# Two attention blocks on one core: projections as rounds of four 32-column tiles, a scheduler with measured waits, GpSimd joins of up to four groups, patterns shifted downwards

## The chip, the core and the metric

The kernel runs on one core of one Trainium2 chip. The metric is the device time of one execution in microseconds (us), as the median of several runs. One execution was also taken with the hardware profiler; all rows below come from it. Engine names: PE is TensorE (matmuls; "PEld" its weight loads), ACT is ScalarE, DVE is VectorE, POOL is GpSimd, SP issues DMAs.

## What is computed

Two independent blocks, each on a sequence of 2048 rows with 512 features, 32 heads of width 16; their outputs are set side by side.

```python
qkv = (x @ wqkv).reshape(B, S, 3, H, Dh).transpose(2, 0, 3, 1, 4)   # S=2048, H=32, Dh=16
# block A, linear attention
phi = lambda t: jnp.where(t > 0, t + 1, jnp.exp(t)) + 1e-6
kv  = einsum("bhsd,bhse->bhde", phi(k), v);  z = sum of phi(k) over s
o   = (phi(q) @ kv) / (phi(q) @ z + 1e-6)
# block B, softmax attention
o   = softmax(q @ k.T * Dh**-0.5) @ v
# each: o in (B, S, D) @ wo;  result = concatenate([a, b], axis=-1)
```

Nearly all the time is block B: 32 heads times 2048 x 2048 scores, an exponential of each.

## The kernel before

**Units and blocks.** The heads of B are handled in 32 units: four head groups Gp, four stretches c of 512 queries, and two halves e_ of the group's heads, so that a unit holds four heads (g = 0 to 3). A unit has 64 blocks, one for each of 16 key tiles j and four heads g: 128 keys by 512 queries. There are 2048 blocks in all. For each one PE computes the scores (`qk`, L871, a matmul with 32 rows of the array, so up to four with different g run side by side), something makes the exponential, and PE multiplies the result with the values (L1253, 128 rows and a tile of 32 columns of the array, of which 17 are used: 16 value columns and a column of ones that gives the softmax's denominator). Four such matmuls with different g also run side by side; such a set is called a round.

**Two ways to the exponential.** The ACT way: PE writes two or three blocks into the PSUM tile pS, and one ACT instruction (L1084) writes their exponentials as fp16 into PT. The integer way: PE writes one block into a bank of pD (or the fifth bank of pS), and DVE (L987) makes an int16 of it, `score * ESC + EB`, whose bits read as fp16 are a rough exponential. Two more patterns are made of it by adding constants (`SHIFT`), 328 for pattern 1 and 656 for pattern 2. The weighted sum of the three is a good exponential, and PE makes it: three value matmuls for each block in place of one, pattern 0 with values multiplied by `VW` (tile VX), patterns 1 and 2 with the plain values VV. Blocks of the integer way are collected in groups of two (1024 columns; eight group buffers of the tile DI). Patterns 1 and 2 of a group are made by GpSimd (`on_pool`, L1176), where up to two waiting shifts are joined in one instruction; with both a pattern 1 and a pattern 2 in it, the pattern 2 is made of the group's finished pattern 1, with 328. Pattern 2 is made by DVE instead (`on_dve`, L1141) when GpSimd's backlog is long.

**The jobs.** Beside this run the projections of B (`proj_job` L600, `v4_job` L677), all of block A (`ak_job` and `av_job` L718, `aq_job` L755, `akvsum_job`, `aden_job`, `anum_job`), the two output projections (`omm_job` L809) and checks of the input's size (`gram_x`, `gram_w`, `flag_job`). The function `halves` cuts the matmuls of a job in two parts of equal length that are placed one by one. All use the full 128x128 array. Their PSUM results are evicted by DVE, or go through an exponential on ACT (L693) and two DVE instructions.

**The order.** Everything is one static program. When it is written, a list scheduler runs through a simulated time: it holds a clock `T` for each engine, a duration for each operation, latencies between engines (`LAT`, 0.12 us, and `LPE`), and always emits the candidate that can start first, by priorities. `fill_act_cand` offers the score matmuls for the next ACT instruction, `fill_d_cand` those for the integer way, `pv_cand` up to `PVR` rounds of value matmuls at once, `job_cand` a part of a job. A PE candidate is dropped if it would end after the time at which the next ACT fill has to start. How many blocks go the integer way is a result of this: a block goes there whenever a bank, a group buffer and the backlogs of DVE and GpSimd allow. The table `SEG` sets 25 parameters of the scheduler anew every 12 us of simulated time (windows, thresholds, priorities, a seed). The chip executes each engine's list in the emitted order, with semaphores where one engine needs another's result.

Of the kernel before, what the change touches and what calls it, by code (L numbers as in the profile page):

```python
# [238 lines left out]
def bass_concat_heads__linear_attn_block__softmax_full_mha__prompt_kernel(nc, A_x, A_wqkv, A_wo, B_x, B_wqkv, B_wo, out):  # L239
# [18 lines left out]
    VW = 1.5546875  # L258
    SHIFT = (328, 656)
    PMX = 0.0  # L260
# [64 lines left out]
    )  # L325
    GB = 0.0
    PM = -0.1
# [28 lines left out]
    EB = 13125.0  # L356
# [3 lines left out]
    with es:  # L360
# [164 lines left out]
        LAT = 0.12  # L525
        LPE = {"dve": 0.04, "act": 0.19, "pool": 0.0, "pe": 0.12, "dma": 0.12}
# [6 lines left out]
        class Shared(float):  # L533

            pass

# [8 lines left out]
        class Job:  # L545
# [11 lines left out]
            def stage_done(self, i, end, bk, bi):  # L557
# [3 lines left out]
                for st, tk in self.gives:  # L561
                    if st == i:
                        tok[tk] = end + LAT
                if i + 1 < len(self.stages):
                    eng, dur, fn = self.stages[i + 1]
                    lat = LAT if eng != "pe" or eng != self.stages[i][0] else 0.0
                    push(eng, end + lat, self.prio if eng == "pe" else (0 if eng == "act" or i + 1 <= self.rel and self.bank else min(self.prio, 2)), dur,
                         lambda st_, en_, fn=fn: (fn(bk), self.stage_done(i + 1, en_, bk, bi)))
# [10 lines left out]
        MM = 0.26  # L579
# [4 lines left out]

        def halves(fn, reads, n=4, parts=2, dur=MM):

            def mk(lo, hi):
                def f(e, bk):
                    for i in range(lo, hi):
                        ins = fn(e, bk, i)  # L590
# [896 lines left out]
        def fill_in(st):  # L1487
# [4 lines left out]
            if n <= 0:  # L1492
                return
# [188 lines left out]
```

## Time and profile before

| | before |
|---|---|
| runs | 661.0, 661.37, 660.76 us; median 661.0 |
| profiled execution | 660.98 us, span from first to last instruction 659.2 us |
| granted TensorE clock | 0.999 |
| ACT exponentials of B (L1084) | 648 instructions: 575 of two blocks, 73 of three, so 1369 blocks |
| integer way (L987) | 492 blocks from pD and 187 from pS, so 679 blocks |
| pattern shifts on GpSimd (L1176) | 198 of 128x2048, 169 of 128x1024, 2 of 128x512 |
| pattern shifts on DVE (L1141) | 113 |
| DMA | 21.53 MB in 53213 packets, mean 33 GB/s |

A row of a group reads: line, engine, operation, output <- input with shapes, count | busy time of the group in us, mean ns of one | idle time of the engine just before them and what ended it. A row of the timeline reads: start and length in us, engine, line, operation, tiles, count; like instructions that follow each other are merged, and the length is then from the first's start to the last's end. The records of PE, DVE and ACT contain the time to the last write, so that the next instruction starts before the record of the last has ended: the pace of an engine is read from the distance of starts, not from the mean length.

### The profile page before, as it was taken

What the parts mean: (1) busy time and instruction counts of PE and PEld (TensorE: products, weight loads), DVE (VectorE), ACT (ScalarE), POOL (GpSimd) and SP (SyncE); (2) the same over time, 40 slices, a digit from 0 to 9 for tenths busy, and PEclk for the clock granted to TensorE, in tenths of its full rate; (3) what the DMA queues carried; (4) which work ended last, traced back from release to release, by engine and by line L of the source; (5) the groups of instructions that cost most, each with busy time, mean ns of one, the idle gap of its engine ahead of it and who ended that gap; (6) DMA issues with size and microseconds to landing.
All of it is one profiled execution on the core that took longest, in us unless ns stands there. A gap on an engine that the chain in (4) does not pass through costs nothing.

```text
span 659.2 us, 15950 instructions
## 1 busy us (share of the span) xinstructions
PE 633.3 (96%) x6609; PEld 200.4 (30%) x6662; DVE 632.1 (96%) x1089; ACT 644.7 (98%) x686; POOL 592.7 (90%) x450
## 2 busy tenths in 40 slices
PE   8999999999999999999999999999999999999997
PEld 6323333222333333332222233322222223232222
DVE  4999999999999999999999999999999999999995
ACT  6999999999999999999999999999999999999994
POOL 5999999999999999999998899999999999999983
PEclk9999999999999999999999999999999999999999
DMA  9701010020102101210012011010011000120102
GB/s 178 207 3 33 1 34 6 11 43 9 34 2 33 21 14 33 65 34 9 9 27 64 17 34 34 18 19 10 7 26 41 17 1 11 25 26 25 33 26 67
DMA packets 53213, 21.53 MB, mean 33 GB/s; under 512 B 44177, under 2 KB 52625, under 8 KB 53137
## 3 DMA queue, kind: packets, MB, share of 16 engines
q1 hardware_dynamic: 51664, 19.80, 13.9%
q8 instruction: 54, 0.88, 0.6%
q10 hardware_dynamic: 1472, 0.66, 0.4%
q14 instruction: 23, 0.18, 0.1%
HBM read 4.46 MB, written 4.19 MB: 13 GB/s over the span
## 4 chain that ended last, share of the span: by engine, by line
ACT 96%; PE 3%; DMA 1%; ACTq 0%; issue 0%; DVE 0%; DVEq 0%
ACT PT L1084 93%; ACT EA L693 2%; DMA Wb<-in_B_wqkv_dram 1%; PE pPV L1253 1%; PE pD L809 1%; PE pS L871 0%; PE pD L1305 0%; PE pS L1305 0%; PE pS L1389 0%; ACTq L442 0%; PE pD L1389 0%; DVE KNa L582 0%; PE pD L659 0%; PE pD L871 0%; DVEq L1626 0%
## 5 line engine op out<-in xcount | busy, mean ns | idle before, releaser
L1084 ACT ACTIVATE PT<-pS 128x1024 f16<-128x1024 f32 (+1 forms) x648 | 636.6, 1305 | 1.0 <-PE pS L871 1.0
L1176 POOL TENSOR_SCALAR DI<-DI 128x2048 int16<-128x2048 int16 (+1 forms) x369 | 554.4, 1503 | 47.3 <-DVE DI L987 20.2
L987 DVE TENSOR_SCALAR DI<-pD 128x512 int16<-128x512 f32 x492 | 324.4, 679 | 6.1 <-PE pD L871 2.5
L871 PE MATMUL pS<-QT,KM 32*128 32x512 bf16 x1556 | 255.0, 384 | 8.8 <-ACT PT L1084 4.5
L1253 PE MATMUL pPV<-PT,VV 128*17 128x512 f16 x1369 | 233.7, 381 | 0.0
L1253 PE MATMUL pPV<-DI,VV 128*17 128x512 f16 x1358 | 227.3, 382 | 0.0
L871 PE MATMUL pD<-QT,KM 32*128 32x512 bf16 x492 | 170.5, 384 | 0.3 <-DVE PQT L696 0.3
L1253 PE MATMUL pPV<-DI,VX 128*17 128x512 f16 x679 | 161.0, 381 | 0.2 <-DVE OT L1282 0.2
L871 PEld LDWEIGHTS pS<-QT,KM 32*128 32x128 bf16 x1556 | 64.6, 91 | 265.3 <-ACT PT L1084 227.4
L987 DVE TENSOR_SCALAR DI<-pS 128x512 int16<-128x512 f32 x187 | 126.6, 677 | 0.7
L1141 DVE TENSOR_SCALAR DI<-DI 128x1056 int16<-128x1056 int16 x113 | 77.0, 687 | 0.5
L1253 PEld LDWEIGHTS pPV<-PT,VV 128*17 128x17 bf16 x1369 | 47.5, 88 | 41.4 <-issue 36.1
L1253 PEld LDWEIGHTS pPV<-DI,VV 128*17 128x17 bf16 x1358 | 47.0, 88 | 40.4 <-issue 33.0
L871 PEld LDWEIGHTS pD<-QT,KM 32*128 32x128 bf16 x492 | 40.5, 91 | 5.4 <-DVE DI L987 2.0
L1253 PEld LDWEIGHTS pPV<-DI,VX 128*17 128x17 bf16 x679 | 34.2, 88 | 22.0 <-issue 17.7
L718 PE MATMUL pD<-Wa,xTa 128*128 128x256 bf16 x200 | 30.5, 275 | 0.3 <-DVE DI L987 0.2
L600 PE MATMUL pD<-xTb,Wb 128*128 128x512 bf16 x67 | 21.2, 383 | 3.1 <-issue 2.3
L1282 DVE STREAM_TRANSPOSE OT<-pPV 128x512 f32<-128x512 f32 x31 | 21.9, 705 | 0.1
L582 DVE CAST KNa<-pD 128x512 bf16<-128x512 f32 x27 | 18.4, 681 | 3.0 <-PE pD L809 2.0
L1288 POOL TENSOR_TENSOR OT<-OT,ZR 128x256 bf16<-128x256 f32 x31 | 19.3, 621 | 1.6
L718 PEld LDWEIGHTS pD<-Wa,xTa 128*128 128x128 bf16 x200 | 15.4, 97 | 13.3 <-issue 6.3
L693 ACT ACTIVATE EA<-pD 128x512 bf16<-128x512 f32 x23 | 19.2, 835 | 0.0
(136 smaller groups left out, 346.3 us busy)
## 6 DMA issues: line engine op xcount, KB each, us to landing
out_dram<-KNa SPq DMA_DIRECT2D x31, 128.0 KB, 1.7
Wa<-in_A_wqkv_dram SPq DMA_DIRECT2D x1, 1536.0 KB, 8.2
KM<-KR SPq DMA_DIRECT2D x96, 16.0 KB, 1.8
Wb<-in_B_wqkv_dram SPq DMA_DIRECT2D x2, 384.0 KB, 4.5
Wb<-in_B_wqkv_dram SPq DMA_DIRECT2D x1, 512.0 KB, 4.6
Wa<-in_A_wo_dram SPq DMA_DIRECT2D x1, 512.0 KB, 4.5
Wa<-in_B_wo_dram SPq DMA_DIRECT2D x1, 512.0 KB, 3.7
ON<-in_B_x_dram ACTq DMA_DIRECT2D x1, 256.0 KB, 3.1
```

The costliest lines, as they stand in the source:

```text
L582: return lambda e, bk: (e.tensor_copy(out_fn(), in_fn(bk)) if lane == "dve" else e.activation(out_fn(), in_fn(bk), ACTF.Copy))
L600: return e.matmul(f32v(bk), lhsT=Wb[:, cc, kind * 512 + Gp * 128:kind * 512 + Gp * 128 + 128], rhs=xTb[:, cc, sc * 512:(sc + 1) * 512], st ...
L693: ("act", 0.052 + n * 0.000833, f_ev("act", lambda e, bk: e.activation(EA[:, 0:n], f32v(bk)[:, c0:c0 + n], ACTF.Exp), [], ["EA"])),
L718: return e.matmul(f32v(bk)[:, 256 * tt:256 * tt + 256], lhsT=xTa[:, b, cc, (o + tt) * 128:(o + tt + 1) * 128], rhs=Wa[:, cc, 512 * kind + ...
L871: return e.matmul(dst, lhsT=KM[32 * g:32 * g + 32, Gp % 2, e_, j * 128:(j + 1) * 128], rhs=QT[32 * g:32 * g + 32, Gp % 2, c * 512:(c + 1) ...
L987: sch.add("dve", lambda e: e.tensor_scalar(DI[:, di_at(0, buf) + i * 512:di_at(0, buf) + (i + n) * 512], f32v(DBANK[b0], n * 512), ESC, EB ...
L1084: sch.add("act", lambda e: e.activation(PTf[:, p0 * 512:p0 * 512 + w], S5[:, c0:c0 + w], ACTF.Exp, scale=SC), reads=skeys(sl, len(bl)), wr ...
L1141: sch.add("dve", lambda e: e.tensor_scalar(gapped(DI, di_at(v, buf), wide // 32, 32), DI[:, di_at(0, buf) - 32:di_at(0, buf) + w], 1.0, fl ...
L1176: sch.add("pool", lambda e: e.tensor_scalar(dv, sv, 1.0, sh_, op0=ALU.mult, op1=ALU.add), reads=keys, writes=[("DI", v_, x) for x, v_ in s ...
L1253: sch.add("pe", lambda e, g=g, j=j, c0=c0, V_=V_, r2=r2, P=P, first=first, last_=last_: e.matmul(PVb[32 * g:32 * g + 17, 0:512] if len(P.s ...
L1282: sch.add("dve", lambda e: e.transpose(OT[:, 0, :], PVb[:, 0:512]), reads=[("PV", g) for g in range(4)], writes=[("OT", 0)])
L1288: ("pool", 0.7, f_op("pool", lambda e: e.tensor_tensor(xn[:, :, 16 * e_:16 * e_ + 16], o[:, :, 0:16], zr.unsqueeze(2).broadcast_to([128, 1 ...
```

## The change

1. **Projections in rounds.** `proj_job`, `ak_job`, `av_job`, `aq_job` and `omm_job` issue each matmul as four with 32 output columns each, at the four column tiles of the array; they are placed in four parts in place of two, and the scheduler counts them as of one kind with the value matmuls. `v4_job`, `gram_x`, `gram_w`, `flag_job`, `akvsum_job`, `aden_job`, `anum_job` and the last outputs stay as they were.
2. **Scheduler's costs.** Latencies are given for each pair of engines, a change of PE's kind of tile costs `SWT`, and the durations are new: 0.214 for a score round, 0.218 for a value or projection round (before 0.215, with 0.1 more after a change; a projection matmul 0.26), 0.157 + 0.000834 for each column for a GpSimd shift (before 0.276 + 0.00083). A fill for ACT has to start 0.43 before ACT runs dry; other PE work may delay it by `KSL`, 0.02. A second round of value matmuls is not added if it would delay the fill. Dummy matmuls fill PE's idle time only from 0.8 us on.
3. **GpSimd joins.** Up to four groups whose buffers lie at equal distances are shifted by one instruction, always from pattern 0 and all for the same pattern. Group buffers are handed out in turn, where before the one longest free was taken.
4. **Patterns downwards.** Pattern 0 is made with `EB` larger by 3072 (eight times the value), VX is divided by eight, and patterns 1 and 2 come from it with -2744 and -2416, which gives the same patterns 1 and 2 as before.
5. **The order.** All rows of `SEG` are new (54 in place of 49), so the whole emitted order differs.

```diff
-    VW = 1.5546875
-    SHIFT = (328, 656)
+    VW = 1.5546875 / 8
+    SHIFT = (-2744, -2416)
...
-    PM = -0.1
+    PM = 0.09
+    JN = 4
+    KSL = 0.02
+    PFX = 0.157
+    FIDLE = 0.8
...
-    EB = 13125.0
+    EB = 13125.0 + 3072.0
...
-        LAT = 0.12
-        LPE = {"dve": 0.04, "act": 0.19, "pool": 0.0, "pe": 0.12, "dma": 0.12}
+        LPE = {"dve": 0.136, "act": 0.426, "pool": PM, "pe": 0.2, "dma": 0.12}
+        LTO = {("pe", "dve"): 0.2, ("pe", "act"): 0.215, ("act", "dve"): 0.4, ("dve", "pool"): 0.163, ("pool", "dve"): 0.07, ("dve", "act"): 0.15}
+        SWT = 0.106
...
+        def pe_at(md):
+
+            return T["pe"] + (0.0 if pmode[0] in (md, None) else SWT)
...
-        MM = 0.26
+        MM = 0.218
...
+            def matmul(self, out_, lhsT, rhs, start, stop):
+                for g in range(4):
+                    ins = self.e.matmul(out_[32 * g:32 * g + 32], lhsT=lhsT[:, 32 * g:32 * g + 32], rhs=rhs, start=start, stop=stop,
+                                        tile_position=(0, 32 * g))
+                return ins
...
-            st = halves(mm, [("Wb", kind, Gp)] + [("xTb", t) for t in range(4 * sc, 4 * sc + 4)])
+            st = halves(mm, [("Wb", kind, Gp)] + [("xTb", t) for t in range(4 * sc, 4 * sc + 4)], parts=4, quad=True)
...
-            start = max(T["pe"], t0, afree[sl] + LAT, pw[0] - 0.5)
-            dur = 0.33 if pmode[0] != "q" else 0.23
+            start = max(pe_at("q"), t0, afree[sl], pw[0] - 0.43)
+            dur = 0.214
...
+                    best = [buf]
+                    for step in range(1, NDG):
+                        run_ = [buf]
+                        while len(run_) < JN and run_[-1] + step in near_:
+                            run_.append(run_[-1] + step)
...
-                        T["pool"] = en_ = st_ + 0.276 + 2 * w * 0.00083
+                    T["pool"] = en_ = st_ + PFX + len(best) * w * 0.000834
...
+                    if rounds > 1 and t_ + 0.218 * rounds > win[0]:
+                        break
...
-                lim = max(dry - fa[1] - LAT - 0.05, fa[0])
+                lim = max(dry - 0.43, fa[0])
```

More of the change, by code (lines that the diff above doesn't have):

```diff
@@ L593, in halves @@
             w = n // parts
-            return [("pe", w * dur, mk(i * w, (i + 1) * w)) for i in range(parts)]
+            return [("pe", Rounds(w * dur) if quad else w * dur, mk(i * w, (i + 1) * w)) for i in range(parts)]
         krc = [0]
@@ L636, in gram_x @@
             ts = range(4 * t4, 4 * t4 + 4)
-            return Job(halves(mm, [("xTb", t) for t in ts], n=16, parts=2, dur=0.07) +
+            return Job(halves(mm, [("xTb", t) for t in ts], n=16, parts=2, dur=0.0555) +
                        [("dve", 0.6, f_ev("dve", lambda e, bk: e.tensor_reduce(GRX[:, t4:t4 + 1], f32v(bk), axis=AX.X, op=ALU.max), [], [("GRX", t4)]))],
@@ L679, in v4_job @@
             ts = range(4 * t4, 4 * t4 + 4)
-            st = halves(mm, [("Wb", 2)] + [("xTb", t) for t in ts], n=16, parts=2, dur=0.07)
+            st = halves(mm, [("Wb", 2)] + [("xTb", t) for t in ts], n=16, parts=2, dur=0.0555)
             st.append(("dve", 0.6, f_ev("dve", lambda e, bk: e.tensor_copy(
@@ L702, in chunked @@
         def chunked(st, i):
-            eng, dur, fn = st[1]
+            eng, dur, fn = st[3]
             def done(bk):
@@ L938, in d_pick @@
             if not dgroup["open"]:
-                buf = min((i for i in range(NDG) if dgfree[i] is not None), key=lambda i: dgfree[i], default=None)
+                buf = min((i for i in range(NDG) if dgfree[i] is not None), key=lambda i: (dgfree[i] > at, (i - dgroup["buf"] - 1) % NDG), default=None)
                 if buf is None or dgfree[buf] > at:
@@ L1066, in run @@
                     tk.append(d_take(pk))
-                if len(bl) + len(tk) > 4:
-                    en += 0.21
+                en = st + 0.214 * max(sum(x[2] == g for x in bl + [y[0] for y in tk]) for g in range(4))
+                T["pe"] = en
+                en = st + 0.214 * max(sum(x[2] == g for x in bl) for g in range(4))
                 c0 = 0 if sl == 0 else 1024 if ax else 1536
@@ L1110, in run @@
                     tk.append(d_take(pk2))
+                    if tk[0][0][2] == tk[1][0][2]:
+                        T["pe"] = en = en + 0.214
                 d_emit(tk, en)
-            return at, 0.32 if pmode[0] != "q" else 0.22, run
+            return at, 0.214, run
         def close_group():
@@ L1166, in on_pool @@
-                    mixed = len({v_ for _, v_ in segs}) == 2
-                    moves = sorted((di_at(1 if mixed and v_ == 2 else 0, b_), di_at(v_, b_)) for b_, v_ in segs)
+                    near_ = {x[1]: x for x in pshift if x[0] == v and x[2] == w and x[3][0] <= st_ + PMW}
+                    best = [buf]
[3 more added lines that the diff above has]
+                            run_.append(run_[-1] + step)
+                        while len(run_) < JN and run_[0] - step in near_:
+                            run_.insert(0, run_[0] - step)
+                        if len(run_) > len(best):
+                            best = run_
@@ new lines, in on_pool @@
+                    keys = []
+                    for b_ in best:
+                        x = near_.get(b_, me[0])
+                        pshift.remove(x)
+                        if b_ != buf:
+                            cands["pool"].remove(x[3])
+                            st_ = max(st_, x[3][0])
+                        keys += [("DI", 0, b_, i) for i in range(n)]
+                    T["pool"] = en_ = st_ + PFX + len(best) * w * 0.000834
+                    moves = [(di_at(0, b_), di_at(v, b_)) for b_ in best]
@@ L1172, in view @@
                             return one
-                        return bass.AP(one.tensor, one.offset, [list(one.ap[0]), [offs[1] - offs[0], 2], [1, w]])
+                        return bass.AP(one.tensor, one.offset, [list(one.ap[0]), [offs[1] - offs[0], len(offs)], [1, w]])
                     sv, dv = view([m_[0] for m_ in moves]), view([m_[1] for m_ in moves])
-                    sh_ = float(SHIFT[0] if mixed else SHIFT[v - 1])
+                    sh_ = float(SHIFT[v - 1])
                     sch.add("pool", lambda e: e.tensor_scalar(dv, sv, 1.0, sh_, op0=ALU.mult, op1=ALU.add),
-                            reads=keys, writes=[("DI", v_, x) for x, v_ in segs])
-                    for x, v_ in segs:
-                        if v_ == 1:
-                            dgroup["st"][x]["v1"] = en_
-                        pv_give[x, v_](en_)
+                            reads=keys, writes=[("DI", v, x) for x in best])
+                    for x in best:
+                        pv_give[x, v](en_)
                 pv_give[buf, v] = lambda en_: give(buf, v, "pool", en_)
@@ L1462, in job_cand @@
             best = None
-            bi = min((i for i in range(NB + JX) if dfree[i] is not None), key=lambda i: (max(dfree[i], T["pe"]), i), default=None)
+            bi = min((i for i in range(NB + JX) if dfree[i] is not None), key=lambda i: (max(dfree[i], pe_at("j")), i), default=None)
             for lst, pr in ((urgent, 0.5), (early, 2), (bjobs, 2.2), (urgent2, 2.3), (ajobs, AJP)):
@@ L1540, in bass_concat_heads__linear_attn_block__softmax_full_mha__prompt_kernel @@
                 opts.append((fa[0], 0, "pe", fa[1], fa[2], None))
+            win[0] = 1e9
+            if fa is not None and nfill[0] >= 2:
+                win[0] = max(T["act"] + sum(exps) - 0.43, fa[0]) + KSL - SWT
             fd = fill_d_cand()
```

131 lines of the change are left out of this document (57 added, 74 removed), and 103 rows, old and new, of the table SEG.

## The prediction

> **What bounds the kernel now.** I read the busy times first, then the chain that ended last.
>
> ```profile
> PE 633.3 (96%) x6609; PEld 200.4 (30%) x6662; DVE 632.1 (96%) x1089; ACT 644.7 (98%) x686; POOL 592.7 (90%) x450
> ACT 96%; PE 3%; DMA 1%; ACTq 0%; issue 0%; DVE 0%; DVEq 0%
> 544.01 94.47 ACT PT L1084 x97
> 638.93 0.54 PE pPV L1253 x8
> ```
>
> All engines look full, but the chain (second row; then two of its pieces) is ACT: exponentials until 638.5 us, then PE. The next rows, from the timeline of ACT and the groups by form, give ACT's pace and amount.
>
> ```profile
> 8.73 37.01 ACT L1084 ACTIVATE PT<-pS 128x1536 f16<-128x1536 f32 x37 [1.05 <-PE pS L871]
> 376.99 3.91 ACT L1084 ACTIVATE PT<-pS 128x1024 f16<-128x1024 f32 x4
> 380.61 0.78 ACT L693 ACTIVATE EA<-pD 128x512 bf16<-128x512 f32 x1
> 381.09 4.89 ACT L1084 ACTIVATE PT<-pS 128x1024 f16<-128x1024 f32 x5
> 645.84 3.94 ACT L1084 ACTIVATE PT<-pS 128x1536 f16<-128x1536 f32 x3
> L1084 ACT ACTIVATE PT<-pS 128x1024 f16<-128x1024 f32 x575 | 560.5, 1260 | 0.0
> L1084 ACT ACTIVATE PT<-pS 128x1536 f16<-128x1536 f32 x73 | 121.5, 1664 | 1.0 <-PE pS L871 1.0
> ```
>
> Four instructions of two blocks take 380.61 - 376.99 = 3.62 us, **0.905 each**; an instruction of block A takes 381.09 - 380.61 = 0.48. One of three blocks is 1664 - 1260 = 404 ns longer, 1.31. With 575, 73 and the 32 of block A (one for each of its 32 key and query jobs) that is 520 + 96 + 15 = 631 us of work. The stretch from 8.73 to 645.84 + 3.94 = 649.8 has 641. So ACT waits for about 10 us in it. ACT can only end earlier if it gets **fewer blocks** (0.905 / 2 = 0.45 us each) or waits less. Its blocks go to the integer way, if the three engines of that way have room.
>
> DVE:
>
> ```profile
> L987 DVE TENSOR_SCALAR DI<-pD 128x512 int16<-128x512 f32 x492 | 324.4, 679 | 6.1 <-PE pD L871 2.5
> L987 DVE TENSOR_SCALAR DI<-pS 128x512 int16<-128x512 f32 x187 | 126.6, 677 | 0.7
> L1141 DVE TENSOR_SCALAR DI<-DI 128x1056 int16<-128x1056 int16 x113 | 77.0, 687 | 0.5
> 309.24 1.29 DVE L987 TENSOR_SCALAR DI<-pD 128x512 int16<-128x512 f32 x2
> 310.44 0.69 DVE L1141 TENSOR_SCALAR DI<-DI 128x1056 int16<-128x1056 int16 x1
> 311.05 0.68 DVE L987 TENSOR_SCALAR DI<-pD 128x512 int16<-128x512 f32 x1
> ```
>
> Two conversions are 1.29 long with records of 0.68, so 0.61 apart; a shift on DVE starts 311.05 - 310.44 = 0.61 before the next. So 679 blocks and 113 shifts are 483 us of DVE's 632, which is full: each block that is moved needs 0.60 there, and each shift that GpSimd takes over gives it 0.61.
>
> GpSimd is the least busy engine, at 90%. Its rows:
>
> ```profile
> L1176 POOL TENSOR_SCALAR DI<-DI 128x2048 int16<-128x2048 int16 x198 | 376.3, 1900 | 28.1 <-DVE DI L987 13.9 <-POOL DI L1176 2.0 <-DVE RD L770 0.2
> L1176 POOL TENSOR_SCALAR DI<-DI 128x1024 int16<-128x1024 int16 x169 | 176.9, 1047 | 18.2 <-DVE DI L987 6.3
> 301.27 2.17 POOL L1176 TENSOR_SCALAR DI<-DI 128x1024 int16<-128x1024 int16 x2
> 303.41 0.65 POOL L684 TENSOR_SCALAR VX<-VV 128x544 bf16<-128x544 bf16 x1
> 311.81 3.88 POOL L1176 TENSOR_SCALAR DI<-DI 128x2048 int16<-128x2048 int16 x2 [0.40 <-DVE DI L987]
> 315.65 0.62 POOL L1288 TENSOR_TENSOR OT<-OT,ZR 128x256 bf16<-128x256 f32 x1
> POOL DI L1176 <- DVE DI L987: 20.2, 54, 1.0
> ```
>
> The records are 1900 and 1047 ns: 1024 columns more are 0.853, and a record holds 0.193 beside them. The starts tell more. Of the pair at 301.27 the second starts 2.17 - 1.05 = 1.12 after the first, a gap of 0.08; but VX (303.41) starts 0.03 before the second's end (303.44). The pair at 311.81 has (3.88 - 3.80) 0.08 between, and L1288 starts 0.04 before its end (315.69). By the order in which the kernel writes them, the second of each pair is a pattern 2, shifted by 656; the first is a pattern 1, shifted by 328. So an instruction costs 0.853 for each group plus **0.27** after a 328 and plus **0.155** where a 656 is followed by another kind.
>
> PE, from its timeline:
>
> ```profile
> 302.32 0.39 PE L871 MATMUL pS<-QT,KM 32*128 32x512 bf16 x3
> 302.64 0.60 PE L600 MATMUL pD<-xTb,Wb 128*128 128x512 bf16 x2
> 303.23 0.39 PE L871 MATMUL pS<-QT,KM 32*128 32x512 bf16 x2
> 303.55 0.39 PE L1253 MATMUL pPV<-DI,VX 128*17 128x512 f16 x1
> 303.78 0.38 PE L1253 MATMUL pPV<-PT,VV 128*17 128x512 f16 x2
> 641.44 0.38 PE L809 MATMUL pD<-Wa,ON 128*128 128x512 bf16 x1 [0.16 <-issue]
> PEld pPV L1253 <- issue: 86.8, 377, 0.4
> ```
>
> Two projection matmuls of 512 columns are 0.60 long with records of 0.38: 0.22 apart, and value rounds are 303.78 - 303.55 = 0.23 apart, so a projection matmul on the full array and a round cost the same. From a score round to what follows it are 0.32. It streams 512 columns too, 0.22, so a change of the array's kind of tile costs about 0.10; the last row has 377 such changes, with loads idle for 0.23 at each. A cycle of two ACT blocks (score round, change, others, change) therefore has 0.905 - 0.22 - 2 x 0.10 = 0.485: **two slots** of 0.22; a cycle of three has 0.89: four. That is 575 x 2 + 73 x 4 = 1442 slots. Needed are (1369 + 3 x 679) / 4 = 851.5 full value rounds; by the code's loops 120 + 112 + 64 = 296 matmuls of 512 columns in the projections, 256 of 256 (128 slots), and about 128 slots of narrower ones: 1404, or 97%. PE is a second bound, with 38 slots to spare for rounds that aren't full.
>
> **The change part by part.**
>
> *GpSimd.* Two savings. First the gap: 0.27 - 0.155 = 0.117 on each of 369 instructions, 43 us, if the new constants behave as 656 does. The trace has no shift by a negative constant. Bounds: 0 (all as after 328) and 43 us (all as after 656); a gain below nothing is excluded only in so far as no row shows a longer gap. Both new constants are far from 328, and pattern 2 has the same shape, type and source, so I take the 656 row; but in these rows the constant and the target's place in DI go together, and if it's the place, the gap stays. Second the joins: now 198 x 2 + 169 + 1 = 566 group shifts in 369 instructions, 1.53 each. Four may be joined, but of one pattern and at equal distances, within the same waiting window; between 1.53 and 4 I take 2.2, nearer to the row. A join makes the first group wait: four groups are 4 x 0.853 + 0.157 = 3.57 us long, where two now take 1.98, and hold four of the eight buffers. What waits is PE's value matmuls of those patterns; the scheduler places them after the pattern's reckoned end and keeps some 22 to 36 others in stock (the table's tenth column), which hide it. Without that stock DVE finds no free buffer and ACT gets the blocks back.
>
> The Trainium skill, GPSIMD Engine Reference, section 2.1 Instruction dispatch, says that a core starts the next Pool instruction as soon as it has finished its share of the last. The rows at 303.41 and 315.65 agree, the pairs with 328 don't. By the rule alone there would be no gap to remove; the joins would save 57 - 40 = 17 us, and the sum would be 656.
>
> Let a be the blocks moved to the integer way and b the shifts that GpSimd takes from DVE, t the change of time.
> - ACT: t = -0.4525 a - w, w the waits removed.
> - DVE: 0.60 a - 0.61 b = t.
> - GpSimd: before 0.274 x 369 = 101 us of fixed cost, after 0.157 (566 + a + b) / 2.2 = 40.4 + 0.071 (a + b), so 0.925 (a + b) - 60.7 = t.
>
> *Measured waits.* The order's durations come closer to the rows: a projection matmul was reckoned at 0.26 (row: 0.22), a score round at 0.23 to 0.33 (0.21 plus 0.10 for each change). Fewer of ACT's 10 us of waits should remain; between 0 and 10 I take w = 3.3, a third, since the fill may now be late by 0.02 and margins (0.12 + 0.05) are gone.
>
> With w = 3.3 the equations give b = 62.0 - 1.49 a and 1.96 a = 34.5: **a = 18, b = 35, t = -11.3**. DVE keeps some 78 shifts.
>
> *Projections.* Their PE time stays: 0.22 for a matmul or for a round of four. What goes is the change when they follow a value round, and pieces are now one slot, so a lone value round and a projection round share a cycle. The row at 641.44 shows what this fills: one projection matmul alone in its cycle. Demand after: 36 more value matmuls, 9 slots; 9 cycles fewer, 18 slots less: 1413 of 1424, 99%. So the gain rests on fuller cycles. The rounds bring four times the instructions, (296 + 256) x 3 = 1656 matmuls and loads more; a round of value matmuls issues four in 0.22 already. Rounds of 256 columns have half of 0.22, an estimate by columns: at best that holds, at worst they take a full 0.22, 256 x 0.11 = 28 us of PE. I take nothing: issue is hidden while the array streams.
>
> *Downward constants* on DVE and VX: the same instructions, no cost. *Buffers in turn, no dummies below 0.8 us*: PE's longest wait for ACT is 0.7 us and the granted clock was full, so I cost both at nothing; that cover is gone if PE's waits reach some us.
>
> ```profile
> PEld pS L871 <- ACT PT L1084: 227.4, 522, 0.7
> PEclk9999999999999999999999999999999999999999
> ```
>
> *Start and end.* ACT's start at 8.73 hangs on loads that stay. After 649.8 the last outputs need 9.4 us to the span's end; unchanged. Between:
>
> ```profile
> 640.00:650.00 10.00, 9.68 (x98) 3.17 (x99) 7.08 (x14) 9.78 (x9) 6.88 (x10) 1.00 0.08 28
> ```
>
> Here DVE and POOL are at 71 and 69% and ACT still waits at times, so a better end is part of w.
>
> Sum: 661.0 (the profiled run, 660.98, is the median of the three) - 11.3 = **649.7**, said as 650.
>
> **The rivals.**
> 1. *GpSimd's gap stays (slower).* The order then reckons 0.157 where 0.274 is paid: (566 + 53) / 2.2 = 281 instructions x 0.117 = 33 us late in all. Its list is in fixed order; value matmuls wait in PE's queue for the pattern, score matmuls stand behind them, and ACT runs dry. Idle in the plan absorbs some: GpSimd has 28.1 + 18.2 = 46 us idle before the shifts now, 20 of them waits for DVE, and will have less. If half comes through, 650 + 16 = **666**. It decides once the planned idle between shifts is below 0.117 each. For it: constant and place can't be told apart. Against: the 656 rows.
> 2. *PE stays the bound.* If cycles aren't filled better than now, 1404 of 1442, a can't be above nothing, and only w is won: **657**.
> 3. *The lateness eats the gain.* 640 fills late by up to 0.02 are 13 us: **662 to 663**, no gain. For it: ACT has no slack between instructions. Against: the row of 0.905 shows fills in time.
> 4. *Narrow rounds cost a full slot.* The 256 rounds of 256 columns then take 256 slots in place of 128, with 11 free: 117 x 0.22 = 26 us, **676**. Against it, the loads of value rounds are hidden: rounds are 0.23 apart with four loads each. The Trainium skill, TensorEngine Tiling (Array Packing), section Restrictions and Gotchas, says that column tiling excludes Fast Weight Load; by that rule this would be the way, and no row here shows a round of 256 columns.
>
> **How the numbers follow.** Forecast 0.58, rival 1 0.16, rival 2 0.15, rival 3 0.07, rival 4 0.04. Predicted 650. Range: low, with w = 10 and joins of 3, the equations give a = 16 and t = -17, so 644, and less if more ACT fills take three blocks (each such cycle has four slots): 639. High: rival 1, 666. A measurement of this kernel tells about 0.2% from no change, 1.3 us: faster is the forecast and rival 2, 0.73; the same, half of rival 3 and a little of the forecast's edge, 0.05; slower the rest, 0.22.
>
> **What would show it.** ACT blocks near 1350 in place of 1369, DVE shifts near 80, GpSimd instructions near 280, and pairs of shifts whose starts are 0.85 for each group plus 0.157 apart: step one right. Plus 0.27: rival 1, with PE waiting for GpSimd. ACT's stretch minus its work: the waits. Rounds of 256 columns 0.11 apart: rival 4 wrong. It is wrong if ACT's blocks don't fall, or fall while waits grow by as much.

## The result and the profile after

The changed kernel takes 696.2 us (median of four runs, 695.4 to 697.1) against 661.2 us for the kernel before (four runs, 660.8 to 661.5): a ratio of 1.053, 95% interval 1.051 to 1.055. The change costs 35 us where 11 were to be gained.

The busy times and the chain that ended last, from the page of the changed kernel:

```profile
span 694.5 us, 19303 instructions
PE 656.4 (95%) x8322; PEld 213.8 (31%) x8322; DVE 625.7 (90%) x1079; ACT 645.5 (93%) x691; POOL 633.3 (91%) x483
POOL 46%; DVE 28%; PE 21%; issue 3%; ACT 2%; DVEq 0%
```

The work of DVE and ACT is a little under or at what it was; the span is longer, so everything waits. The chain, 96% ACT before, now runs through GpSimd. The groups by form, then the waits, say what came of each step:

```profile
L1111 ACT ACTIVATE PT<-pS 128x1024 f16<-128x1024 f32 x604 | 574.4, 1117 | 27.3 <-PE pD L899 13.9 <-PE pS L899 12.7
L1111 ACT ACTIVATE PT<-pS 128x1536 f16<-128x1536 f32 x49 | 75.0, 1531 | 5.1 <-PE pS L899 4.4 <-PE pD L899 0.6
L1203 POOL TENSOR_SCALAR DI<-DI 128x2048 int16<-128x2048 int16 x191 | 363.0, 1901 | 15.0
L1203 POOL TENSOR_SCALAR DI<-DI 128x1024 int16<-128x1024 int16 x205 | 214.7, 1047 | 19.1 <-DVE DI L1015 3.9
L1203 POOL TENSOR_SCALAR DI<-DI 128x3072 int16<-128x3072 int16 x6 | 16.5, 2753 | 0.5
L1170 DVE TENSOR_SCALAR DI<-DI 128x1056 int16<-128x1056 int16 x87 | 58.8, 685 | 0.2
```
```profile
PEld pPV L1281 <- POOL DI L1203: 33.8, 63, 1.7
PE pPV L1281 <- POOL DI L1203: 13.4, 25, 1.2
```

ACT has 604 x 2 + 49 x 3 = 1355 blocks, 14 fewer than before, and DVE 87 shifts in place of 113. So work did move to the integer way, about three quarters of the amount that I had worked out (18 blocks, 35 shifts). GpSimd makes 191 x 2 + 205 + 6 x 3 = 605 group shifts in 402 instructions, 1.50 in each: before it was 1.53. And PE, which in the kernel before waited 0.9 us for GpSimd in its loads (the row below, from the groups by form of before), now does so 63 times in its loads (33.8 us) and 25 times in its matmuls (13.4 us).

```profile
L1253 PEld LDWEIGHTS pPV<-DI,VV 128*17 128x17 bf16 x1358 | 47.0, 88 | 40.4 <-issue 33.0 <-POOL DI L1176 0.9 <-DVE DI L1141 0.7
```

Rows of the timelines show how GpSimd keeps time (the first), and where ACT starts and ends (the other two):

```profile
104.20 2.17 POOL L1203 TENSOR_SCALAR DI<-DI 128x1024 int16<-128x1024 int16 x2
```
```profile
8.85 5.97 ACT L1111 ACTIVATE PT<-pS 128x1536 f16<-128x1536 f32 x5 [1.05 <-PE pS L899]
657.94 24.05 ACT L1111 ACTIVATE PT<-pS 128x1536 f16<-128x1536 f32 x21 [0.26 <-PE pD L899]
```

The second shift of the pair starts 2.17 - 1.05 = 1.12 after the first. The order reckoned 0.157 + 0.854 = 1.01. The gap of 0.08 after a record that I had read as the mark of the constant 328 is there with the new constants too, and not in this pair alone: in 397 of the 402 shifts the next instruction starts within 0.15 us of the record's end, 0.08 after it on the mean. ACT's stretch is 681.99 - 8.85 = 673.1 us. Its work, by the paces of the prediction, is 604 x 0.905 + 49 x 1.31 + 15.4 = 626 (before 631), so its waits went from 10 to 47 us. After its end there are 12.5 us to the end of the span (before 9.4). Together: -5 + 37 + 3 = 35 us.

### The profile page after: what moved, and what is told of

The parts are those of the page before. It is cut to its first block, busy times and chain, and to the rows that moved or that the text cites. A ratio compares the mean times of both kernels' runs of the same rounds, so it can differ in the third digit from the quotient of the medians.

```text
span 694.5 us, 19303 instructions
## 1 busy us (share of the span) xinstructions
PE 656.4 (95%) x8322; PEld 213.8 (31%) x8322; DVE 625.7 (90%) x1079; ACT 645.5 (93%) x691; POOL 633.3 (91%) x483
## 3 DMA queue, kind: packets, MB, share of 16 engines
q1 hardware_dynamic: 51664, 19.80, 13.2%
## 4 chain that ended last, share of the span: by engine, by line
POOL 46%; DVE 28%; PE 21%; issue 3%; ACT 2%; DVEq 0%
POOL DI L1203 43%; DVE DI L1015 19%; PE pPV L1281 7%; PE pS L899 6%; PE pD L609 4%; DVE DI L1170 2%; POOL OT L1316 2%; ACT PT L1111 2%; DVE OT L1310 1%; DVE ON L1321 1%; DVE KNa L595 1%; PE pS L609 1%; POOL VX L712 1%; DVE PQT L724 1%; PE pD L1394 1%
## 5 line engine op out<-in xcount | busy, mean ns | idle before, releaser
L1203 POOL TENSOR_SCALAR DI<-DI 128x1024 int16<-128x1024 int16 (+1 forms) x402 | 594.2, 1478 | 34.6 <-DVE DI L1015 3.9
L899 PE MATMUL pS<-QT,KM 32*128 32x512 bf16 x1558 | 263.1, 386 | 6.0 <-DVE DI L1015 2.5
L1281 PE MATMUL pPV<-DI,VV 128*17 128x512 f16 x1386 | 243.6, 387 | 14.0 <-POOL DI L1203 13.4
L1281 PE MATMUL pPV<-PT,VV 128*17 128x512 f16 x1355 | 239.0, 385 | 0.0
L1015 DVE TENSOR_SCALAR DI<-pS 128x512 int16<-128x512 f32 x203 | 137.7, 678 | 4.9 <-PE pS L899 4.9
L1170 DVE TENSOR_SCALAR DI<-DI 128x1056 int16<-128x1056 int16 x87 | 58.8, 685 | 0.2
L899 PEld LDWEIGHTS pD<-QT,KM 32*128 32x128 bf16 x490 | 41.8, 91 | 13.2 <-DVE DI L1015 8.2
L609 PE MATMUL pD<-Wa,xTa 128*32 128x256 bf16 x832 | 34.4, 275 | 0.4 <-DVE DI L1015 0.4
L609 PE MATMUL pD<-xTb,Wb 128*32 128x512 bf16 x368 | 29.2, 385 | 0.3 <-DVE DI L1015 0.2
L609 PEld LDWEIGHTS pD<-Wa,xTa 128*32 128x32 bf16 x832 | 18.1, 95 | 13.6 <-issue 8.2
L1321 DVE STREAM_TRANSPOSE ON<-OT 128x512 bf16<-128x512 bf16 x12 | 8.5, 711 | 14.1 <-POOL OT L1316 14.1
```

What stands on the lines that cost most here:

```text
L609: ins = self.e.matmul(out_[32 * g:32 * g + 32], lhsT=lhsT[:, 32 * g:32 * g + 32], rhs=rhs, start=start, stop=stop, tile_position=(0, 32 * g))
L899: return e.matmul(dst, lhsT=KM[32 * g:32 * g + 32, Gp % 2, e_, j * 128:(j + 1) * 128], rhs=QT[32 * g:32 * g + 32, Gp % 2, c * 512:(c + 1) ...
L1015: sch.add("dve", lambda e: e.tensor_scalar(DI[:, di_at(0, buf) + i * 512:di_at(0, buf) + (i + n) * 512], f32v(DBANK[b0], n * 512), ESC, EB ...
L1170: sch.add("dve", lambda e: e.tensor_scalar(gapped(DI, di_at(v, buf), wide // 32, 32), DI[:, di_at(0, buf) - 32:di_at(0, buf) + w], 1.0, fl ...
L1203: sch.add("pool", lambda e: e.tensor_scalar(dv, sv, 1.0, sh_, op0=ALU.mult, op1=ALU.add), reads=keys, writes=[("DI", v, x) for x in best])
L1281: sch.add("pe", lambda e, g=g, j=j, c0=c0, V_=V_, r2=r2, P=P, first=first, last_=last_: e.matmul(PVb[32 * g:32 * g + 17, 0:512] if len(P.s ...
```

## The experiments

My theory after these rows: GpSimd's shifts cost 0.27 beside their columns as before, the order believes 0.157, and its list falls behind the others. Several experiments use the order's own end: the largest of the scheduler's clocks when all is emitted, 647.2 us for the kernel before (measured 661.2, so 14.0 late) and 646.1 for the changed kernel (696.2, so 50.1 late). (The expectation of experiment 9 takes ACT's clock alone, 646.4 and 645.6.) The rivals were the downward constants as such, the rounds, and the thinner margins and missing dummies.

### 1. The right price in the changed kernel

```diff
-    PFX = 0.157
+    PFX = 0.274
```

> The changed kernel with one number undone: the scheduler reckons 0.274 us of fixed cost for a GpSimd shift (as the trace of the changed kernel shows) in place of 0.157; all instructions have the same forms, only the order and the counts follow. Theory 1 (GpSimd's gap stayed, the order was written for a faster GpSimd, and the late patterns stall PE and then ACT): most of the 35 us come back; its lists hold 657 ACT instructions with 1373 blocks, some 633 us of ACT work, so with 10 to 20 us of waits 660 to 672 us. PE's waits for GpSimd fall from 47 us to under 10. Rival (the rounds of narrow matmuls or the smaller margins before an ACT fill cost the time): 685 us or more.

Measured: 678.6 us, ratio 1.026 (1.024 to 1.027). 17.6 of the 35 us came back with one number of the order, and the time lies between the theory's 660 to 672 and the rival's 685. ACT leads the chain again, and PE's waits for GpSimd in its loads are small:

```profile
ACT 84%; PE 12%; DVE 1%; DMA 1%; issue 0%; DVEq 0%
PEld pPV L1281 <- POOL DI L1203: 2.3, 10, 0.2
```

Why the other half stayed is read from the order's own clock. This version ends there at 662.6, the changed kernel's order at 646.1: the same number made the order itself longer by 16.5. Measured against that clock it is 678.6 - 662.6 = 16.0 late, near the 14.0 of the kernel before and far from 50.1. So the right price takes away nearly all of the lateness, and what it leaves is a longer order.

One stretch stood out in this trace. The windows give span, busy time and count for PE, PEld, DVE, ACT and POOL, then the granted clock, the DMA share and GB/s:

```profile
30.00:38.00 8.00, 7.02 (x77) 1.72 (x73) 8.00 (x14) 8.00 (x10) 7.25 (x7) 1.00 0.02 4
38.00:46.00 8.00, 6.72 (x60) 2.11 (x62) 3.10 (x6) 5.76 (x7) 2.73 (x3) 0.55 0.00 0
46.00:54.00 8.00, 8.00 (x72) 1.32 (x64) 5.15 (x10) 5.11 (x6) 4.23 (x5) 0.60 0.01 3
36.30:38.80 2.50, 1.46 (x7) 0.37 (x7) 2.46 (x5) 2.50 (x4) 2.38 (x3) 1.00 0.00 0
38.80:52.50 13.70, 12.83 (x101) 2.92 (x101) 6.50 (x11) 8.80 (x10) 6.16 (x7) 0.50 0.01 2
```

From 36.3 us on PE had score rounds alone in their cycles, 1.46 us of work in 2.5. Then the granted clock stood at 0.50 for 13.7 us, to 52.5.

### 2. Upward constants again

```diff
-    VW = 1.5546875 / 8
-    SHIFT = (-2744, -2416)
+    VW = 1.5546875
+    SHIFT = (328, 656)
-    EB = 13125.0 + 3072.0
+    EB = 13125.0
```

> The changed kernel with the patterns made upwards again (328 and 656, the old base and VW); the order is the same, instruction by instruction. Theory 1: the constants are not what costs the time; gaps next to 656 vanish only beside instructions of other kinds, some 30 places x 0.117 = 3.5 us of GpSimd, so within 0.5% of the changed kernel. Rival (negative constants made each shift slower): 20 us or more faster than the changed kernel.

Measured: 692.8 us, ratio 1.047 (1.046 to 1.049). The downward constants cost 3.5 us, no more. The traces show where: in 30 places a pattern 2 stands before or after an instruction of another kind, and the gap there goes from 0.08 to -0.03, 3.3 us in all, as the expectation had it. So the gap was not something that the change added: most of it had been there before, and had been reckoned with.

### 3. The wrong price alone, in the kernel before

```diff
-                        T["pool"] = en_ = st_ + 0.276 + 2 * w * 0.00083
+                        T["pool"] = en_ = st_ + 0.157 + 2 * w * 0.00083
...
-                    me = [(v, buf, w, push("pool", t_ + LAT + 0.05, 0, 0.276 + w * 0.00083, on_pool), rk)]
+                    me = [(v, buf, w, push("pool", t_ + LAT + 0.05, 0, 0.157 + w * 0.00083, on_pool), rk)]
```

> The kernel before with one number changed: the scheduler reckons 0.157 in place of 0.276 for a GpSimd shift; projections, latencies and constants stay as before. Theory 1: this alone slows the kernel before, 590 group shifts in 414 instructions x 0.117 = 48 us too little reckoned, so 680 to 700 us, with PE waiting for GpSimd for 20 us or more. Rival: GpSimd's slack of 46 us takes it up, 661 to 666 us.

Measured: 697.4 us, ratio 1.055 (1.053 to 1.057). The kernel before with nothing but a wrong belief about GpSimd is as slow as the changed kernel, and looks like it, in its chain (GpSimd first) and its waits:

```profile
POOL 44%; PE 20%; DVE 17%; ACT 12%; issue 4%; DMA 1%; SPq 1%; DVEq 0%; POOLq 0%
PEld pPV L1253 <- POOL DI L1176: 33.0, 64, 1.7
```

The near-equal loss is in part chance. The order that comes of the false price ends at 661.8 by its own clock, 14.6 later than the one of before; its table had been made for the old price, which fits. So of the 36 us some 15 are a longer order and 697.4 - 661.8 - 14.0 = 22 are lateness; in the changed kernel, whose table was made for the false price, all is lateness.

### 4. What sets the gap

GpSimd alone, series of six shifts of 128x1024 with nothing else running, one line for each constant; the outputs are left at zero.

```python
for i in range(6): e.tensor_scalar(PA(i), S(i), 1.0, 328.0, op0=ALU.mult, op1=ALU.add)
```

> Not the reference's computation: GpSimd alone, series of six shifts of 128x1024 int16 with one constant each, in two target tiles, output zeros. Theory (the constant sets the gap): series with 656 start 1.01 us apart whatever the target, series with 328, -2744 and -2416 start 1.11 to 1.13 apart. Rival (the target's place sets it): the spacing goes with the tile. Rival (the gap comes from the neighbours on DVE or from semaphores): all series 1.01 apart here.

The timeline; a row's length is from the first start to the last end of its six, lines 23, 26, 29, 32 and 35 are the constants 328, 656, -2744, -2416 and -656:

```profile
8.85 6.58 POOL L23 TENSOR_SCALAR pa<-src 128x1024 int16<-128x1024 int16 x6
15.65 6.08 POOL L26 TENSOR_SCALAR pa<-src 128x1024 int16<-128x1024 int16 x6
21.87 6.58 POOL L29 TENSOR_SCALAR pa<-src 128x1024 int16<-128x1024 int16 x6
28.67 6.58 POOL L32 TENSOR_SCALAR pa<-src 128x1024 int16<-128x1024 int16 x6
35.48 6.09 POOL L35 TENSOR_SCALAR pa<-src 128x1024 int16<-128x1024 int16 x6
```

(6.58 - 1.05) / 5 = 1.106 us from start to start with 328, and (6.08 - 1.05) / 5 = 1.006 with 656. A second target tile gave the same numbers for 328, 656 and -2416. So the constant sets the gap, and both constants of the change are of the kind that has it.

### 5. Other ways to make the same shift

```python
for i in range(6): e.tensor_scalar(PA(i), S(i), 984.0, -656.0, op0=ALU.add, op1=ALU.add)
```

> GpSimd alone: series of six int16 shifts of 128x1024, the outputs left at zero. In the series before, starts were 1.008 us apart with 656 and 1.107 with 328, whatever the target. New: the sum made from two constants (328 as 984 - 656, 656 - 328, 512 - 184, 1 + 327; 656 as 328 + 328 and 656 + 0), more single constants, and another source value (12797), by which 656 gives the result that 328 gave. Theory A, the constant of the second operation sets the gap: 984 - 656 starts 1.008 apart, 656 - 328 1.107, and the other source value changes nothing. Theory B, the value of the result sets it: all pairs that make 328 are 1.107, and 12797 + 656 is 1.107 too. Theory C, any constant of the two with a gap brings it: 656 - 328, 512 - 184 and 328 + 328 are 1.107, 984 - 656 is 1.008. In the last series 656 and 328 take turns: the start after a 328 comes 0.10 later than the one after a 656, if the gap belongs to the instruction that has just run.

The first of the pairs, the other source value with 656, and the series in which 656 and 328 take turns:

```profile
9.73 21.59 POOL L24 TENSOR_SCALAR pa<-src 128x1024 int16<-128x1024 int16 x6
240.54 6.09 POOL L60 TENSOR_SCALAR pa<-s 128x1024 int16<-128x1024 int16 x6
368.34 6.58 POOL L120 TENSOR_SCALAR pa<-src 128x1024 int16<-128x1024 int16 x6
```

All three theories missed on the pairs: two additions take 3.6 us in place of 1.05 with each of the ten pairs, so this form was useless. (Nine start 3.59 apart and one, 1 + 327, 3.69; several of the nine contain a 328, so the gap doesn't follow the rule of the single constants here.) The source value changes nothing (1.01), as theory A said and B denied. The last row corrects my reading of before: with 656 and 328 in turn *every* start is 1.106 after the last, so the gap lies on both sides of a 328 and doesn't belong to the instruction that has just run; a 656 goes without it beside another 656. The trace of before says the same when its shifts are matched with their constants, in the order in which the kernel writes them. A 656 with the next instruction close behind (within 0.15 us) was followed 84 times by a 328, with a gap of 0.08, and 16 times by another operation, which started 0.04 before its record's end. Those 16 of 369 are what I had taken as the price of a 656.

### 6. The rounds alone

```diff
-                        ins = fn(e, bk, i)
+                        ins = fn(Quad(e) if quad else e, bk, i)
```

> The kernel before, its order and all else kept, with each projection matmul issued as four of 32 columns. Theory, rounds of four are free: 661, within 1.5 us, since PE's stream is as long, ACT sets the end, and the array's changes of tile that go were reckoned with in the order. Rival, narrow rounds cost: the 256 matmuls of 256 columns take a full 0.22 each, 256 x 0.11 = 28 us more of PE, up to 689; or the issue of 1656 more matmuls and loads shows as 2 to 5 us.

Measured: 661.3 us, ratio 1.0003 (0.9993 to 1.0012). Rounds cost nothing, and by themselves bring nothing.

### 7. Dummies in short idle stretches

```diff
-    FIDLE = 0.8
+    FIDLE = 0.0
```

> The changed kernel with GpSimd reckoned at 0.274 (the order of e1_pool_cost, 678.6 us), and dummies in idle stretches of any length again (152 in place of 22). In e1 the granted clock fell to 0.55 between 38 and 46 us and 0.60 between 46 and 54, after a stretch from 36.3 to 40 us in which PE had only score rounds, and the drift against the order jumped by 5 us there. Theory, the missing dummies cost those 5 us: clock 1.00 in that stretch, 673.5 in all. Rival, the stretch is late for another reason, or the dummies themselves come late and hold up PE: 678 or more.

Measured: 677.7 us, ratio 1.025 (1.023 to 1.026), 0.9 us less than experiment 1. The same windows as there:

```profile
30.00:38.00 8.00, 8.00 (x96) 2.24 (x87) 7.99 (x14) 8.00 (x10) 7.41 (x8) 1.00 0.02 4
38.00:46.00 8.00, 8.00 (x100) 3.56 (x98) 4.53 (x8) 6.84 (x8) 3.80 (x5) 1.00 0.01 2
46.00:54.00 8.00, 7.99 (x119) 2.63 (x120) 8.00 (x16) 8.00 (x9) 7.46 (x8) 1.00 0.01 3
```

The clock stays at 1.00, as expected: missing dummies had let it fall. The 5 us were wrong: the profiled execution of experiment 1 was the slowest of its four (680.5, the others 677.4 to 678.6). The medians differ by 0.9, and with 676.9 to 677.9 here the two sets of runs overlap, so whether the dummies gain anything isn't shown. The changed kernel shows no such fall in that stretch (1.00 from 30 to 62 us), but its clock stood at half four times for 3.4 us, from 106, 314, 526 and 649 us on. The first:

```profile
106.00:109.40 3.40, 3.40 (x38) 0.80 (x30) 2.76 (x5) 1.66 (x2) 3.18 (x5) 0.50 0.00 0
```

Its four executions have mean clocks of 0.988 to 0.996 and lie within 1.7 us, the slowest not at the lowest clock, so these falls are no main part of the 35 us; in experiment 9, with the same dummies, the clock is 1.00 from 6 to 657 us.

### 8. A search for constants without the gap

The series of experiment 4 with 75 constants.

> GpSimd alone again, outputs left at zero: series of four int16 shifts of 128x1024 by 75 constants, to learn which ones have the gap and whether a set for this kernel exists without it: the two patterns need constants that are 328 and 656 apart from the base, up to whole octaves of 1024 (328 or -696 or 1352 and 656 or -368 or 1680). Theory A, the gap goes with the constant's size in the sense of the series before (none from 512 to 1023): -696 starts 1.008 apart, and -368 1.107, as -328 and -500. Theory B, the sign or the number's bits decide in another way (400 had none, 300 and 500 had it): then -368 and its neighbours may be without. A set with both at 1.008 would allow the changed kernel's order to run on the price that it reckons with; without one, the price of 0.157 can't be had for both patterns.

Lines 56 and 77 are -384 and -704, four shifts each, line 23 is -368:

```profile
8.85 4.38 POOL L23 TENSOR_SCALAR pa<-src 128x1024 int16<-128x1024 int16 x4
59.06 4.08 POOL L56 TENSOR_SCALAR pa<-src 128x1024 int16<-128x1024 int16 x4
89.68 4.08 POOL L77 TENSOR_SCALAR pa<-src 128x1024 int16<-128x1024 int16 x4
```

(4.08 - 1.05) / 3 = 1.01 for -384 and -704, (4.38 - 1.05) / 3 = 1.11 for -368. Theory A held for the two that it named, yet size alone isn't the rule. Over the three series the constants without the gap are 0 to 3, 32, 64, 100, 128, 200, 256 to 272, 384 to 408 and 512 to 1023, and those with it 4 to 16, 82, 150, 164, 288 to 376, 416 to 511 and all that were tried from 1024 to 4096, the sign without effect where both were tried. A stretch stands for the constants tried in it. Why these, stays open. Pattern 1 at -704 and pattern 2 at -384 are close to 328 and 656 less an octave (-696 and -368), and with another weight for pattern 0 the weighted sum is as even as before (worked out over an octave: 0.21% standard deviation in both).

### 9. The change with constants that have no gap

```diff
-    VW = 1.5546875 / 8
-    SHIFT = (-2744, -2416)
+    VW = 0.77
+    SHIFT = (-704, -384)
-    EB = 13125.0 + 3072.0
+    EB = 14162.0
```

> The changed kernel, its order instruction for instruction, with two constants that had no gap in the series: -704 and -384 in place of -2744 and -2416, and the base and the weight of pattern 0 set to match (14162 and 0.77). GpSimd's starts should then be 0.853 a group plus 0.155 apart, as reckoned. Theory, the gap is the whole loss: the order ends at 645.6 by its own reckoning, and the kernel before needed 14.8 more than its own (646.4, measured 661.2); so 660 to 661, no loss and no gain. Rival, a part of the loss lies in the rounds, the thinner margins or the missing dummies: then 665 or more remains, and PE still waits for GpSimd for more than 10 us or its clock falls somewhere.

Measured: 660.9 us, ratio 0.9995 (0.9985 to 1.0004). The same order as that of the changed kernel, instruction for instruction, and all of the loss is gone. Its page, waits and timelines:

```profile
PE 641.8 (97%) x8321; PEld 205.2 (31%) x8322; DVE 624.4 (95%) x1079; ACT 639.6 (97%) x691; POOL 619.5 (94%) x483
ACT 79%; PE 17%; DVE 2%; DMA 1%; issue 0%
```
```profile
POOL DI L1203 <- DVE DI L1015: 14.3, 35, 1.7
PEld pPV L1281 <- POOL DI L1203: 1.4, 6, 0.3
98.51 2.06 POOL L1203 TENSOR_SCALAR DI<-DI 128x1024 int16<-128x1024 int16 x2
272.21 3.77 POOL L1203 TENSOR_SCALAR DI<-DI 128x2048 int16<-128x2048 int16 x2
8.55 12.38 ACT L1111 ACTIVATE PT<-pS 128x1536 f16<-128x1536 f32 x12 [1.05 <-PE pS L899]
623.38 24.05 ACT L1111 ACTIVATE PT<-pS 128x1536 f16<-128x1536 f32 x21 [0.26 <-PE pD L899]
```

2.06 - 1.05 = 1.01 and 3.77 - 1.90 = 1.87: the reckoned prices, 1.01 and 1.87. PE's waits for GpSimd in its loads fall from 33.8 us to 1.4; GpSimd waits for DVE, and ACT leads the chain. Against the order's own end the kernel is 660.9 - 646.1 = 14.8 late, as the kernel before was (14.0). ACT's stretch is 647.43 - 8.55 = 638.9 us with the same 626 of work, so 12.7 us of waits, 3 more than before. It ends 2.4 us earlier than before (649.8), but the span's end comes 13.2 after that (before 9.4). So the 5 us of work that ACT lost went into waits and the end; the profiled execution was also the slowest of its ten, 1.2 above the median.

### 10. Another table for the true price

The kernel of experiment 7, at 0.274, with a table searched for at that price (55 rows, all other code the same).

> The kernel of e7_dummies_back (GpSimd reckoned at 0.274, the price that it has with the constants of the change; 677.7 us) with another table of 55 rows, found for this price: its order ends at 650.7 by its own reckoning in place of 662.6. Theory, what was left of the loss in e7 is that the table was made for the wrong price: 650.7 + 15 = 665.5. Rival, the reckoned end says little of the measured one when the table is another: 670 to 678.

Measured: 668.0 us, ratio 1.011 (1.009 to 1.013). That lies between theory and rival, nearer the theory. 9.7 of the 16.5 us that were left in experiment 7 went with the table, of 11.9 reckoned. So what experiment 1 didn't bring back was, for the most part, a table made for the wrong price.

### 11. Constants without the gap, and the table searched on

```diff
-        (492.0,0.3,4,3,0,1,6,2,10.0,22,2.5,7.0,1.8,1.8,2,5.0,2.0,2.5,1.0,2,1,0.3,4,0,0,101),
-        (504.0,0.15,4,5,4,1,6,2,12.0,30,2.5,7.0,0.5,1.8,3,5.0,2.0,3,1.5,1,1,0.3,6,20,0,177),
-        (516.0,0.3,4,3,4,1,8,2,12.0,30,3.0,5.0,0.8,1.8,3,5.0,2.0,3,1.5,3,1,0.0,4,14,0,182),
+        (492.0,0.3,4,3,0,1,6,2,10.0,22,2.5,7.0,1.8,1.8,2,5.0,2.0,2.5,1.0,2,1,0.3,4,0,2,30),
+        (504.0,0.15,4,5,4,1,6,2,12.0,30,2.5,7.0,0.5,1.8,3,5.0,2.0,3,1.5,1,1,0.3,6,20,2,19),
+        (516.0,0.3,4,3,4,1,8,2,12.0,36,3.0,4.0,0.8,1.8,3,5.0,2.0,3,1.5,3,1,0.0,4,14,0,182),
...
```

> The kernel of e9_gapfree (660.9 us) with the table searched on at the true price: five rows more or other, the reckoned end 644.8 in place of 646.1, all else equal. Theory, the reckoned end carries over: 660.9 - 1.3 = 659.6, 0.2 to 0.3% under the kernel before. Rival, so small a difference is lost in waits that the order doesn't know: 660.5 to 661.5, no difference.

Measured: 658.0 us, ratio 0.9953 (0.994 to 0.997): faster than both kernels, and by more than reckoned. The span and ACT's last row:

```profile
span 655.6 us, 19291 instructions
616.59 29.55 ACT L1112 ACTIVATE PT<-pS 128x1024 f16<-128x1024 f32 x27 [0.23 <-PE pD L900]
```

ACT ends at 646.1, 1.3 before experiment 9, as reckoned; and the end after it is 9.5 us, as in the kernel before, in place of 13.2. The rest of the gain is there. (The two profiled executions are 4.3 us apart, the medians 2.9.)

## Why the prediction was wrong

**The step that failed** is GpSimd's first saving: "0.27 - 0.155 = 0.117 on each of 369 instructions, 43 us, if the new constants behave as 656 does". (The figures before rounding are 0.274 and 0.157.) They behave as 328 does (experiment 4): two shifts start 1.12 apart where the order has 1.01, and with constants that have no gap the same order takes 660.9 in place of 696.2. I gave both bounds, 0 and 43 us, and took the upper one because the 656 row had the same shape and source. But that row was one of 16: by experiment 5 a 656 beside a 328 has the gap as well, so the 0.155 stood for a neighbourhood and not for an operation. The saving was 0, the lower bound, and since the order had been made with 0.157 for every shift, the price that wasn't saved came back as lateness.

**Rival 1 was right in mechanism and too small in size.** It said what came: the order reckons 0.157, 0.274 is paid, PE waits for the pattern with the scores behind it, ACT runs dry. I priced it at 281 instructions x 0.117 = 33 us and let half come through. There were 402 instructions, so 47 us too little in the order, and 696.2 - 660.9 = 35.3 came through (experiment 9 differs from the changed kernel by the constants, the base and the weight alone). The idle time that was to absorb it was in the plan already: where an order packs all engines to 94% and more, a lateness of one is a lateness of all. Rival 1 should have had the larger chance, and its price most of 47.

**Joins.** Estimated at 2.2 groups an instruction, they came to 1.50, no more than before. Put 1.50 into the prediction's own three equations, with no waits removed: the fixed cost becomes 0.104 for each group shift, and a = 13.7, b = 24, t = -6. Measured are 14 blocks moved, 26 shifts taken from DVE, and 5 us less work on ACT. So the equations give the counts once the joins are right; the 2.2 was wrong. Even without the gap the change would then have given 655 at best, and it gave 660.9; the difference is in ACT's waits and the end.

**Measured waits.** I took 3.3 of ACT's 10 us as removed. With the gap out of the way (experiment 9) ACT waits 12.7, so this term has the other sign, and the unchanged end that I had assumed became 3.8 us longer in that order. By experiment 11 a few rows of the table remove the longer end. Nor did the measured costs bring the order's clock nearer to the chip: 14.0 us late before, 14.8 in experiment 9.

**Rounds.** Costed at nothing: right, as far as the time goes (experiment 6). Rounds of 256 columns, in the changed kernel:

```profile
121.93 0.62 PE L609 MATMUL pD<-Wa,xTa 128*32 128x256 bf16 x16
```

Four rounds of four take 0.62 with records of 0.27, so they are about 0.11 apart: rival 4 was wrong. The Trainium skill's rule that I had set beside it (TensorEngine Tiling (Array Packing), Restrictions and Gotchas: no Fast Weight Load in column tiling) shows no price here; the loads lie beside the streams. **Rivals 2 and 3** can't be judged in the changed kernel. In experiment 9 PE is 97% busy and ACT still leads the chain, so rival 2's bound isn't reached there. Its waits grew by 3 us net, where rival 3 had 13 us of late fills; how much of the 12.7 is late fills isn't shown.

**Downward constants** I costed at nothing; they took 3.5 us (experiment 2). That is about what the gap is worth in the 30 places where -2416 has it and 656 has not. **Dummies** I costed at nothing too, "gone if PE's waits reach some us": in the order of experiment 1 the clock was at half for 13.7 us, but no cost of it stands out of the runs.

The Trainium skill's sentence (GPSIMD Engine Reference, section 2.1 Instruction dispatch: the next Pool instruction starts as soon as a core has finished its share) agrees with a series of shifts by 656, at 1.01, and not with one by 328, at 1.11. The prediction had set it beside rows of both kinds; it says nothing of a constant that decides.

## What to carry to other kernels

A duration in a hand-made order is a claim on the hardware: measure it with the operands that will run, constants and neighbours included, before the order is searched on it, since an order that believes 0.117 us too little of a full engine's 402 instructions lost 35 us. Compare the time with the order's own end, too: it tells lateness (a false price) from a longer order (a table that doesn't suit the price). When a row carries a term only under a condition (this constant, next to that instruction), count how often the condition holds before multiplying: here in 16 of 369. And price a lateness by what the whole packed order loses, not by the idle time of the late engine.

## What the runs showed of the hardware

- GpSimd's int16 shift of 128x1024 starts 1.01 or 1.11 us after the one before, by the value of the constant in it and in its neighbour (experiments 4, 5 and 8; the neighbour tried with 328 and 656); two source values and two target tiles made no difference.
- The operations of a GpSimd instruction can weigh more than its size. At 128x1024 in int16 multiply and add take 1.05 us, one addition alone 2.77 (the row below), two additions 3.63 (experiment 5); multiply and add on 128x3072 take 2.75.

```profile
L110 POOL TENSOR_SCALAR pa<-src 128x1024 int16<-128x1024 int16 x6 | 16.4, 2768 | 0.1
```

- PE's granted clock fell to 0.50, for 13.7 us, after 2.5 us with nothing but score rounds, 1.46 us of work (experiment 1), and stayed at 1.00 where dummy matmuls filled the same stretch (experiment 7).
